# Pooled attention and a top-1 expert layer: a third of a tile between a transfer and its first split

## The chip, the cores and the metric

The kernel runs on one core of one Trainium2 chip. A core has TensorE (PE in the profile), VectorE (DVE), ScalarE (ACT), GpSimd (POOL) and SyncE (SP, which here only issues DMAs). Each of them works through its own queue in order, and waits at an instruction whose inputs or buffers aren't ready. The metric is the device time of the kernel in microseconds. Before the change the median of three runs is 2689.65 us (2684.49 to 2690.37).

## The reference

```python
def _attn_ref(q, kv, w_sr):                     # q: 4 x 12288 x 128, kv: 4 x 384 x 32 x 128
    kv_pool = kv.reshape(B, H // 4, 4, W // 4, 4, C).mean(axis=(2, 4))
    k = v = kv_pool.reshape(B, -1, C) @ w_sr    # 768 keys a batch, which are the values too
    s = (q @ k.transpose(0, 2, 1)) / np.sqrt(C)
    a = np.exp(s - s.max(-1, keepdims=True))
    a /= a.sum(-1, keepdims=True) + 1e-09
    return a @ v

def _moe_ref(x, w_gate, w1, w2):                # x: the 49152 rows above, 8 experts, 128 -> 1024 -> 128
    logits = x @ w_gate
    expert_idx = np.argmax(logits, axis=1)
    ...
    for e in range(E):
        mask = expert_idx == e
        h = np.maximum(x[mask] @ w1[e], 0.0)
        out[mask] = gate_w[mask, None] * (h @ w2[e])
    return out
```

`gate_w` is the softmax of the logits at the chosen expert.

## The kernel before

The 49152 query rows are worked off in 96 tiles of 512 rows, 24 a batch. To keep float32 accuracy every matmul is done as three in the type float32r (`mm3`, lines 219 to 221): each operand is split into a high part (a cast, `high`, line 213, on ACT) and a low part (source minus high, `low`, line 216, on DVE or POOL).

A tile goes through these steps:

- `load` (SP, four DMAs, line 685) and `turn_q` (DVE) bring the queries in and transpose them; `high_q` (ACT) and `low_q` (POOL) split them.
- Four times, for 128 rows each: `scores` (PE, 768 columns, into one of two places in PSUM in turn, so that it needs the exponential of the scores two before), `maxima` (DVE, line 719), `exps` (ACT, line 730), `turn_p` (DVE, 32 x 32 blocks transposed, line 742, into `pb`).
- `move_p` (SP, four DMAs, line 752) finishes the transposition of the probabilities by moving blocks between partitions, from `pb` to `pt`. There are two `pt` buffers, so the transfer of tile i waits for the last `values` matmul of tile i-2 as well as for the last `turn_p` of its own tile.
- Three times, for a third of the keys each: `high_p` (ACT, tile `pth`, 128 x 1024) and `low_p` (POOL, into `pt` itself).
- `values` 0 to 5 (PE), accumulated in one bank, of which 0 and 1 need the first third, 2 and 3 the second, 4 and 5 the last. `high_x` (ACT) and `low_x` (DVE) split the result, `xh` and `xl`.
- `logits` (PE), `diag` (ACT, tile `lgd`), and for pairs of tiles a row of small instructions on DVE, POOL and ACT for the choice of the expert and the gate (`route`; `df` at line 408, `dn` at 434, `se` at 448, `sx` at 461, `sb` at 475).
- Eight times: `first` (PE, an eighth of the hidden units, in one of three free banks), `high_h` (ACT, a relu, tile `hh`, three buffers), `low_h` (DVE, tile `hlow`), `second` (PE, accumulated in one bank).
- `turn_y` (DVE), `scale_y` (POOL, tile `yo`) and `put` (SP, four DMAs, line 904).

All rows of a batch first go through the expert that most rows of its first tile chose. For three of the four batches POOL scatters the row numbers to lists by indirect DMA (line 664), and two passes near the end work off 128 rows each of the other experts. While a batch runs, the keys of the next are pooled, projected and split, in six tiles of its 24 (`keys`; 18 such tiles for batches 1 to 3).

The order on PE, ACT, DVE and POOL is written out by numbers. Each step of tile i is recorded at a time 16 i + an offset, the program is emitted in the order of these times, and each engine's queue has that order. The offsets are in `AT` (line 30); they set an order only, and one unit is a sixteenth of a tile. An offset such as 34.98 therefore means that `values` 0 of a tile stands among the work of two tiles later. SP isn't in that order by hand: a scheduler places its DMAs.

Of the kernel before, what the change touches and what calls it, by code (L numbers as in the profile page):

```python
# [27 lines left out]


AT = {  # L30
    "turn_q": -17.69, "high_q": -7.6, "low_q": -5.97, "maxima": 1.36, "exps": 2.18, ("scores", 0): -0.86,
    ("scores", 1): 3.8, ("scores", 2): 7.89, ("scores", 3): 12.08, ("first_p", 0): 6.32, ("first_p", 1): 4.1,
    ("first_p", 2): 4.74, ("first_p", 3): 5.1, ("first_p", 4): 5.32, ("first_p", 5): 7.4, "first_high": 0.5,
    "first_low": 1.3, "first_values": 2.69, "turn_p": 2.9, "move_p": 17.32, ("high_p", 0): 20.23,
    ("high_p", 1): 22.63, ("high_p", 2): 24.99, "low_p": 1.26, ("values", 0): 34.98, ("values", 1): 37.95,
    ("values", 2): 38.94, ("values", 3): 39.96, ("values", 4): 45.78, ("values", 5): 47.57, "high_x": 0.58,
    "low_x": 1.04, "logits": 3.4, "diag": 3.87, "route": 5.41, "step": 0.4, "scale_exp": 2.92, "scale": 2.84,
    "apart": 7.77, "spread": 9.4, "keep_s": 10.53, ("first", 0): 66.35, ("first", 1): 67.88,
    ("first", 2): 68.93, ("first", 3): 70.9, ("first", 4): 73.89, ("first", 5): 74.05, ("first", 6): 76.9,
    ("first", 7): 78.27, "high_h": 0.48, "low_h": 1.51, "second": 4.29, "turn_y": 0.9, "scale_y": 2.68,  # L40
    "put": 4.98, "cut": -4.95,
}


# [1155 lines left out]
```

## Time and profile before

| | |
|---|---|
| median of three runs | 2689.65 us |
| the profiled execution | 2689.08 us |
| its span, first to last instruction | 2687.4 us |
| instructions | 29654 |
| ACT, idle in front of `pth` | 661.8 us over 279 |
| POOL, idle in front of `pt` | 613.2 us over 279 |
| DMA, mean busy share of q1 (SP's) | 42.4% |
| one `pt` transfer, issue to landing, median | 6.5 us |

The profile names a group of instructions by line, engine and tile, `pth<-pt` being what it writes and what it reads. Idle time of an engine is put down to whoever released it. Times of queues (SPq) are issue times. The granted clock is a share of full speed, for TensorE alone.

### The profile page before, as it was taken

How to read it: one execution, taken by the hardware profiler on the slowest of the kernel's cores; microseconds unless marked ns; L12 is line 12 of the kernel's file. 1: busy time of each engine (PE TensorE's matmuls, PEld its weight loads, DVE VectorE, ACT ScalarE, POOL GpSimd, SP SyncE). 2: the span in 40 equal slices, each digit the busy share in tenths (PEclk: the TensorE clock that was granted, in tenths of full speed). 3: DMA queues.
4: the chain of work that ended last, by engine and by line, in shares of the span. 5: the costliest groups of instructions: out<-in, count | busy, mean ns of one | idle time of the engine just before them, and what ended most of it. 6: DMA issues, size and time to landing. Idle time of an engine off the chain costs nothing.

```text
span 2687.4 us, 29654 instructions
## 1 busy us (share of the span) xinstructions
PE 2220.8 (83%) x9316; PEld 1782.4 (66%) x9316; DVE 1718.2 (64%) x2658; ACT 1332.4 (50%) x2630; POOL 1295.0 (48%) x1157
## 2 busy tenths in 40 slices
PE   3788888788878888878888888887888888887887
PEld 2576766666667676667666667676766767676765
DVE  5565667775666566766576657676667666666654
ACT  2555454555455544545444545554545454554543
POOL 1133454565565545555465545455547454434432
PEclk9898989998989898999889898899888889898998
DMA  7333335444353443554435343544343434435230
GB/s 139 75 75 83 80 78 118 109 98 85 74 123 72 86 79 78 120 109 90 91 87 108 67 92 66 107 112 100 87 92 81 85 72 83 114 71 127 59 83 17
DMA packets 497650, 239.89 MB, mean 89 GB/s; under 512 B 427440, under 2 KB 433714, under 8 KB 497488
## 3 DMA queue, kind: packets, MB, share of 16 engines
q1 hardware_dynamic: 488144, 237.69, 42.4%
q0 software_dynamic: 9344, 0.26, 0.3%
q8 instruction: 74, 1.21, 0.2%
q14 instruction: 88, 0.72, 0.1%
HBM read 59.97 MB, written 31.92 MB: 34 GB/s over the span
## 4 chain that ended last, share of the span: by engine, by line
PE 46%; DMA 23%; SPq 12%; ACT 8%; DVE 6%; issue 4%; POOL 0%; ACTq 0%; DVEq 0%; POOLq 0%
DMA pt<-pb 23%; PE ps L219 16%; PE ps L220 15%; PE ps L221 15%; SPq L752 12%; ACT pth L213 3%; ACT prob L730 3%; ACT hh L863 2%; DVE hlow L867 1%; DVE nmax L719 1%; DVE pb L742 1%; DVE half L256 1%; DVE se L448 1%; DVE df L408 0%; DVE pk L536 0%
## 5 line engine op out<-in xcount | busy, mean ns | idle before, releaser
L216 POOL TENSOR_TENSOR pt<-pt,pth 128x1024 fp32r<-128x1024 f32 x279 | 665.7, 2386 | 613.2 <-ACT pth L213 572.3
L867 DVE SCALAR_TENSOR_TENSOR hlow<-ps,hh 128x512 fp32r<-128x512 f32 x768 | 514.6, 675 | 654.6 <-ACT hh L863 653.6
L213 ACT CAST pth<-pt 128x1024 fp32r<-128x1024 f32 x279 | 293.4, 1052 | 661.8 <-DMA pt<-pb 588.7
L863 ACT ACTIVATE hh<-ps 128x512 fp32r<-128x512 f32 x768 | 451.7, 600 | 309.8 <-PE ps L221 298.3
L219 PE MATMUL ps<-kh,qh 128*128 128x512 f32 (+1 forms) x768 | 290.4, 378 | 302.8 <-ACT prob L730 301.6
L742 DVE STREAM_TRANSPOSE pb<-prob 128x768 f32<-128x768 f32 x372 | 362.0, 973 | 123.7 <-ACT prob L730 115.7
L730 ACT ACTIVATE prob<-ps,nmax 128x768 f32<-128x768 f32 x384 | 355.4, 926 | 132.2 <-DVE nmax L719 131.8
L719 DVE TENSOR_REDUCE nmax<-ps 128x1 f32<-128x768 f32 x384 | 363.1, 946 | 83.1 <-PE ps L221 82.8
L219 PE MATMUL ps<-xh,wt 128*128 128x512 f32 x768 | 329.4, 429 | 91.6 <-DVE hlow L867 85.1
L219 PEld LDWEIGHTS ps<-kh,qh 128*128 128x128 f32 x768 | 156.1, 203 | 365.5 <-ACT prob L730 341.4
L219 PE MATMUL ps<-hh,wt 128*128 128x512 f32 x768 | 336.3, 438 | 3.2 <-ACT hh L863 3.2
L220 PE MATMUL ps<-hlow,wt 128*128 128x512 f32 x768 | 333.8, 435 | 2.4 <-DVE hlow L867 2.4
L221 PE MATMUL ps<-hh,wt 128*128 128x512 f32 x768 | 329.9, 430 | 0.0
L664 POOL DMA_INDIRECT lists<-row,dst x288 | 289.5, 1005 | 55.8 <-issue 51.6
L220 PE MATMUL ps<-xl,wt 128*128 128x512 f32 x768 | 316.1, 412 | 0.0
L221 PE MATMUL ps<-xh,wt 128*128 128x512 f32 x768 | 314.3, 409 | 0.0
L895 POOL TENSOR_TENSOR yo<-yb,sb 128x512 f32<-128x512 f32 x96 | 100.5, 1047 | 443.0 <-DVE yb L890 242.3
L220 PE MATMUL ps<-kl,qh 128*128 128x512 f32 (+1 forms) x768 | 273.4, 356 | 0.0
L221 PE MATMUL ps<-kh,ql 128*128 128x512 f32 (+1 forms) x768 | 272.1, 354 | 0.1
L219 PEld LDWEIGHTS ps<-xh,wt 128*128 128x128 f32 x768 | 158.3, 206 | 137.4 <-DVE hlow L867 93.6
L221 PE MATMUL ps<-pth,vl 128*128 128x512 f32 x558 | 239.7, 430 | 0.0
L219 PE MATMUL ps<-pth,vh 128*128 128x512 f32 x558 | 238.6, 428 | 0.0
(203 smaller groups left out, 3279.2 us busy)
## 6 DMA issues: line engine op xcount, KB each, us to landing
pt<-pb SPq DMA_DIRECT2D x372, 384.0 KB, 6.5
raw<-in_kv_dram SPq DMA_DIRECT2D x96, 256.0 KB, 3.6
qb<-in_q_dram SPq DMA_DIRECT2D x384, 64.0 KB, 2.3
out_dram<-yo SPq DMA_DIRECT2D x384, 64.0 KB, 2.8
raw<-in_moe_w_dram SPq DMA_DIRECT2D x12, 512.0 KB, 4.6
lists<-row,dst POOLq DMA_INDIRECT x288, 2.2
kvs<-kh SPq DMA_DIRECT2D x4, 384.0 KB, 2.3
kvs<-kl SPq DMA_DIRECT2D x4, 384.0 KB, 2.5
```

What stands on the lines that cost most here:

```text
L213: nc.scalar.copy(out=dst, in_=src)
L216: eng.tensor_tensor(out=dst, in0=src, in1=h.bitcast(F32), op=ALU.subtract)
L219: nc.tensor.matmul(out=ps, lhsT=wh, rhs=xh, start=start, stop=False)
L220: nc.tensor.matmul(out=ps, lhsT=wh, rhs=xl, start=False, stop=False)
L221: nc.tensor.matmul(out=ps, lhsT=wl, rhs=xh, start=False, stop=stop)
L664: put = nc.gpsimd.indirect_dma_start(out=lists, out_offset=bass.IndirectOffsetOnAxis(ap=state["dst", b, c][:, n : n + 1].bitcast(U32), axi ...
L719: nc.vector.tensor_reduce(out=nmax, in_=own["s", a], op=ALU.max, axis=AX.X, negate=True)
L730: nc.scalar.activation(out=by_key(prob) if i < FIRST else prob, in_=split_keys(own["s", a]) if i < FIRST else own["s", a], func=AF.Exp, bi ...
L742: nc.vector.transpose(out=own["pb"][:, :, :, a, :].rearrange("p c b t -> p b c t"), in_=own["prob", a].rearrange("p (b c t) -> p b c t", c ...
L752: nc.sync.dma_start(out=dst[:, g], in_=src[g * SQ : (g + 1) * SQ])
L863: nc.scalar.activation(out=hh, in_=own["hp", f], func=AF.Relu)
L867: nc.vector.scalar_tensor_tensor(out=hl, in0=own["hp", f], scalar=0.0, in1=own["hh", f].bitcast(F32), op0=ALU.max, op1=ALU.subtract,)
```

## The change

It changes numbers in `AT` and nothing else; the function bodies and the number of instructions stay. The offsets of the three `high_p` go up by 4.28, 5.05 and 3.79 sixteenths of a tile:

```diff
-    "turn_q": -17.69, "high_q": -7.6, "low_q": -5.97, "maxima": 1.36, "exps": 2.18, ("scores", 0): -0.86,
+    "turn_q": -17.69, "high_q": -7.6, "low_q": -7.35, "maxima": 1.36, "exps": 2.04, ("scores", 0): 0.0,
...
-    "first_low": 1.3, "first_values": 2.69, "turn_p": 2.9, "move_p": 17.32, ("high_p", 0): 20.23,
-    ("high_p", 1): 22.63, ("high_p", 2): 24.99, "low_p": 1.26, ("values", 0): 34.98, ("values", 1): 37.95,
...
+    "first_low": 1.3, "first_values": 2.69, "turn_p": 3.06, "move_p": 17.26, ("high_p", 0): 24.51,
+    ("high_p", 1): 27.68, ("high_p", 2): 28.78, "low_p": 6.6, ("values", 0): 34.68, ("values", 1): 37.36,
```

On ACT, before, in the middle of the program, from the exponential of the first 128 rows of a tile (`prob_11717`) to the last split of the tile ahead (all three splits read `pt_11719`):

```order
L730 ACTIVATE prob_11717,sums_11716<-ps_152,nmax_11709 128x768
L863 ACTIVATE hh_11735<-ps_152 128x512
L385 COPY lgd_11542<-ps_152 32x128 x4
L213 CAST pth_11759<-pt_11719 128x1024
L863 ACTIVATE hh_11761<-ps_152 128x512
L863 ACTIVATE hh_11776<-ps_152 128x512
L730 ACTIVATE prob_11784,sums_11716<-ps_152,nmax_11768 128x768
L213 CAST pth_11795<-pt_11719 128x1024
L863 ACTIVATE hh_11813<-ps_152 128x512
L213 CAST qh_11833<-qt_11686 128x512
L213 CAST pth_11837<-pt_11719 128x1024
```

The same tile on ACT after the change, up to the first of its splits and a little beyond (they read `pt_11709` here, and the other two follow four rows further down):

```order
L730 ACTIVATE prob_11720,sums_11719<-ps_152,nmax_11714 128x768
L863 ACTIVATE hh_11734<-ps_152 128x512
L385 COPY lgd_11541<-ps_152 32x128 x4
L863 ACTIVATE hh_11761<-ps_152 128x512
L863 ACTIVATE hh_11778<-ps_152 128x512
L730 ACTIVATE prob_11782,sums_11719<-ps_152,nmax_11766 128x768
L863 ACTIVATE hh_11799<-ps_152 128x512
L213 CAST qh_11822<-qt_11674 128x512
L213 CAST pth_11824<-pt_11709 128x1024
L863 ACTIVATE hh_11851<-ps_152 128x512
L730 ACTIVATE prob_11853,sums_11719<-ps_152,nmax_11838 128x768
```

The first split stood ahead of the `hh` of expert steps 1, 2 and 3, of the second exponential and of `qh`; now it stands behind them all, and ahead of the `hh` of step 4 and the third exponential.

On POOL, before, from one tile's output rows (`yo`) to the last low part of a tile of probabilities (`pt_10550`):

```order
L895 TENSOR_TENSOR yo_10603<-yb_10581,sb_10567 128x512
L216 TENSOR_TENSOR pt_10550<-pt_10550,pth_10594 128x4x256
L664 DMA lists_75<-row_8116,dst_9711 397312x2
L216 TENSOR_TENSOR pt_10550<-pt_10550,pth_10620 128x4x256
L216 TENSOR_TENSOR ql_10670<-qt_10514,qh_10651 128x512
L664 DMA lists_75<-row_8116,dst_9711 397312x2
L216 TENSOR_TENSOR pt_10550<-pt_10550,pth_10655 128x4x256
```

On POOL after the change, from the gate's `sx` through the low parts of one tile (`pt_10743`) to the output rows:

```order
L461 TENSOR_TENSOR sx_10919<-row_9991,quad_123 128x16 x2
L664 DMA lists_75<-row_8110,dst_9715 397312x2
L216 TENSOR_TENSOR pt_10743<-pt_10743,pth_10858 128x4x256
L216 TENSOR_TENSOR pt_10743<-pt_10743,pth_10906 128x4x256
L664 DMA lists_75<-row_8110,dst_9715 397312x2
L216 TENSOR_TENSOR pt_10743<-pt_10743,pth_10922 128x4x256
L895 TENSOR_TENSOR yo_11021<-yb_11019,sb_10969 128x512
```

The three low parts stood behind `yo`, with the small rows of the gate and `ql` between them; now they stand together, behind `sx` and ahead of `yo`.

On PE, `values` 5 of a tile moves ahead of `second` 5 and of the next tile's `scores` 0, and `values` 4 stands right in front of it; `values` 1 and 2 follow each other, `second` 7 goes behind `values` 0 and `first` 7 ahead of `second` 4. On DVE, `xl` moves from behind the first maximum of a tile to ahead of it, right behind the last `hlow`. On SP, whose rows follow from the others, a piece of the query load now stands between the transfer and the output rows:

```order
L752 DMA pt<-pb 128x1x768 x4
L685 DMA qb<-in_q_dram 32x16x32
L904 DMA out_dram<-yo 32x16x32 x4
L685 DMA qb<-in_q_dram 32x16x32 x3
```

Before, the four pieces of the query load stood together behind the output rows.

More of the change, by code (lines that the diff above doesn't have):

```diff
@@ L30 @@
 AT = {
-    "turn_q": -17.69, "high_q": -7.6, "low_q": -5.97, "maxima": 1.36, "exps": 2.18, ("scores", 0): -0.86,
-    ("scores", 1): 3.8, ("scores", 2): 7.89, ("scores", 3): 12.08, ("first_p", 0): 6.32, ("first_p", 1): 4.1,
+    "turn_q": -17.69, "high_q": -7.6, "low_q": -7.35, "maxima": 1.36, "exps": 2.04, ("scores", 0): 0.0,
+    ("scores", 1): 3.8, ("scores", 2): 8.16, ("scores", 3): 12.5, ("first_p", 0): 6.32, ("first_p", 1): 4.1,
     ("first_p", 2): 4.74, ("first_p", 3): 5.1, ("first_p", 4): 5.32, ("first_p", 5): 7.4, "first_high": 0.5,
-    "first_low": 1.3, "first_values": 2.69, "turn_p": 2.9, "move_p": 17.32, ("high_p", 0): 20.23,
-    ("high_p", 1): 22.63, ("high_p", 2): 24.99, "low_p": 1.26, ("values", 0): 34.98, ("values", 1): 37.95,
[L36 to L41, printed above, removed]
+    "first_low": 1.3, "first_values": 2.69, "turn_p": 3.06, "move_p": 17.26, ("high_p", 0): 24.51,
+    ("high_p", 1): 27.68, ("high_p", 2): 28.78, "low_p": 6.6, ("values", 0): 34.68, ("values", 1): 37.36,
+    ("values", 2): 37.37, ("values", 3): 39.33, ("values", 4): 46.57, ("values", 5): 46.84, "high_x": 0.58,
+    "low_x": 1.04, "logits": 3.4, "diag": 4.52, "route": 6.37, "step": 0.4, "scale_exp": 2.67, "scale": 3.11,
+    "apart": 4.33, "spread": 8.01, "keep_s": 8.68, ("first", 0): 66.2, ("first", 1): 67.88,
+    ("first", 2): 68.9, ("first", 3): 70.6, ("first", 4): 73.48, ("first", 5): 74.05, ("first", 6): 76.52,
+    ("first", 7): 78.07, "high_h": 0.57, "low_h": 1.51, "second": 5.06, "turn_y": 0.97, "scale_y": 1.03,
+    "put": 6.25, "cut": -5.08,
 }
```

## The prediction

> **What bounds the kernel now.** I read the page's busy shares first, then the list of waits, then the chain of work that ended last, then one tile of it in windows.
>
> ```profile
> PE 2220.8 (83%) x9316; PEld 1782.4 (66%) x9316; DVE 1718.2 (64%) x2658; ACT 1332.4 (50%) x2630; POOL 1295.0 (48%) x1157
> ...
> PE 46%; DMA 23%; SPq 12%; ACT 8%; DVE 6%; issue 4%; POOL 0%; ACTq 0%; DVEq 0%; POOLq 0%
> ```
>
> No engine is full, and 35% of the chain is one transfer: the DMA and SyncE's queue (SPq) that issues it. The list of waits says who stands still for it.
>
> ```profile
> ACT pth L213 <- DMA pt<-pb: 588.7, 93, 8.0
> ...
> PE ps L219 <- ACT prob L730: 301.6, 87, 5.7
> PE ps L219 <- DVE hlow L867: 95.9, 21, 6.4
> ...
> POOL sx L461 <- DVE row L452: 16.7, 9, 5.5
> ```
>
> ACT stands 588.7/93 = 6.3 us in front of the first split of nearly every tile (93 of 96 tiles have such a transfer), with its other work queued behind it, and so PE stands 301.6/87 = 3.5 us, mostly in front of scores that need an exponential. One round of the chain shows how this repeats (start, length, what):
>
> ```profile
> 1329.09 0.33 SPq L752
> 1329.46 0.60 SPq L752
> 1330.11 2.39 SPq L752
> 1332.55 6.48 DMA pt<-pb
> 1339.12 1.05 ACT pth L213
> 1340.22 0.47 issue
> 1340.68 0.59 ACT hh L863
> 1341.28 0.89 ACT prob L730 x2
> 1342.21 0.58 PE ps L219
> ```
>
> At 1329.09 the last values matmul of tile i-2 ends and frees the buffer `pt`. Four issues and the transfer take until about 1339.0, that is **9.9 us** after it. Only then may ACT split, relu and exponentiate, and PE goes on at 1342.21. The same round in windows (length, then busy time and count of PE, PEld, DVE, ACT, POOL; then granted clock):
>
> ```profile
> 1329.10:1338.10 9.00, 9.00 (x41) 7.13 (x40) 4.69 (x8) 3.09 (x8) 1.05 (x1) 1.00 0.81 176
> 1338.10:1342.20 4.10, 0.12 (x1) 0.00 (x0) 1.34 (x3) 3.05 (x6) 1.96 (x1) 0.92 0.58 100
> 1342.20:1348.40 6.20, 6.19 (x16) 5.03 (x17) 4.97 (x11) 4.08 (x7) 5.27 (x5) 0.50 0.00 0
> 1348.40:1356.15 7.75, 7.75 (x37) 6.40 (x37) 6.80 (x10) 3.19 (x6) 5.81 (x6) 1.00 0.11 17
> ```
>
> PE is full for 9 us, idle for 4, then full **at half the clock** for 6.2 us (16 matmuls instead of some 30), then full again. The idle time costs twice: itself, and 3.1 us of slow clock behind it. Not every gap does that (idle time in brackets, and the rows behind it):
>
> ```profile
> 133.36 0.58 PE L219 MATMUL ps<-kh,qh 128*128 128x256 f32 x1 [4.21 <-ACT prob L730]
> 342.35 0.38 PE L219 MATMUL ps<-kh,qh 128*128 128x256 f32 x1 [2.70 <-ACT prob L730]
> ...
> 342.81 0.40 PE L219 MATMUL ps<-pth,vh 128*128 128x512 f32 x1
> ```
>
> After 4.21 us the matmul of 256 columns took 0.58 us, after 2.70 us 0.38, and the next one 0.40, its full-clock length. So a tile without this stall takes PE 27.05 - 3.99 - 3.1 = **20.0 us**. The tile interval now is read from the first and last of 92 equal instructions, one a tile (tiles 4 to 95):
>
> ```profile
> 108.28 1.28 POOL L216 TENSOR_TENSOR ql<-qt,qh 128x512 fp32r<-128x512 f32 x1 [16.43 <-ACT qh L213]
> ...
> 2574.50 1.27 POOL L216 TENSOR_TENSOR ql<-qt,qh 128x512 fp32r<-128x512 f32 x1
> ```
>
> 91 intervals in 2466.2 us: 27.10 us each.
>
> **The change, part by part.** It adds and removes no instruction; durations stay those of these groups:
>
> ```profile
> L216 POOL TENSOR_TENSOR pt<-pt,pth 128x1024 fp32r<-128x1024 f32 x279 | 665.7, 2386 | 613.2 <-ACT pth L213 572.3
> L867 DVE SCALAR_TENSOR_TENSOR hlow<-ps,hh 128x512 fp32r<-128x512 f32 x768 | 514.6, 675 | 654.6 <-ACT hh L863 653.6
> L213 ACT CAST pth<-pt 128x1024 fp32r<-128x1024 f32 x279 | 293.4, 1052 | 661.8 <-DMA pt<-pb 588.7
> L863 ACT ACTIVATE hh<-ps 128x512 fp32r<-128x512 f32 x768 | 451.7, 600 | 309.8 <-PE ps L221 298.3
> ...
> L742 DVE STREAM_TRANSPOSE pb<-prob 128x768 f32<-128x768 f32 x372 | 362.0, 973 | 123.7 <-ACT prob L730 115.7
> L730 ACT ACTIVATE prob<-ps,nmax 128x768 f32<-128x768 f32 x384 | 355.4, 926 | 132.2 <-DVE nmax L719 131.8
> L719 DVE TENSOR_REDUCE nmax<-ps 128x1 f32<-128x768 f32 x384 | 363.1, 946 | 83.1 <-PE ps L221 82.8
> ```
>
> And of PE's steps, with six matmuls of 512 columns between these two starts at full clock:
>
> ```profile
> 1329.61 0.39 PE L219 MATMUL ps<-xh,wt 128*128 128x512 f32 x1
> ...
> 1331.01 0.39 PE L377 MATMUL ps<-xh,wgs 128*128 128x512 f32 x1
> ```
>
> 1.40/6 = 0.233 us, so 0.70 for an expert step or a values step, 0.47 for logits, and 1.05 for a scores step (three of 512 and three of 256 columns).
>
> *The first split behind more of ACT's work.* Count PE's new order from V, the end of the last values step, which releases the transfer. Ahead of ACT's split now stand `hh` of expert step 3 and `qh`, and that `hh` takes one of three buffers, freed by second step 0. Until its end PE does second 5, scores 0, second 6, first 0, logits, values 0, second 7, scores 1, first 1 and 2, values 1 and 2, first 3, second 0: eleven steps of 0.70, logits, and two scores: 7.7 + 0.47 + 2.1 = 10.3 us. Then `hh` 0.60 and `qh`, of the same shape, 0.60: the split stands ready at V + 11.5, and its data has been there since V + 9.9. **The wait of 6.3 us goes**, with 1.6 us to spare. Were the data later, ACT has another 0.9 us: the split done at V + 12.5, the `hh` behind it needs first 4, which ends at V + 13.4 (behind values 3, scores 2 and second 1). That `hh` is wanted by second 4 only 4.6 us later, for 1.3 us of `hh` and `hlow`: 3.3 us. PE feels a landing only 5.8 us late. What the landing can do:
>
> ```profile
> DMA to landing us min/median/max: 4.5/6.5/9.2
> ```
>
> 2.7 us late at the most, as measured now. SP's queue changes too: one piece of the q load stands between the transfer and the output rows, and one ahead of the next transfer, 0.6 us of issue by the second row of the chain. Cover: the 5.8 us.
>
> *Transposes ahead of the transfer.* It also waits for the last `pb`. From scores 3 to V, PE has first 6, first 7, second 4, values 4 and 5: 3.5 us. DVE needs the maximum, 0.95, then `hlow` 0.68 and `qt` (by its columns two thirds of a `pb`, 0.65) beside ACT's 0.93 of exponential, then `pb` 0.97: 3.2 us. About equal, and some 1.3 us late where a routing row of that length (`se`, quoted below; every second tile) pushes DVE; same cover.
>
> *What is late next.* `xh` and `xl` of the same V take 0.6 + 0.7 us (shapes of `hh` and `hlow`), but `xl` now stands behind that `pb` and one more `hlow`: at the worst V + 1.3 + 0.7 + 0.7 = V + 2.7, while PE reaches logits at V + 3.15 (second 5, scores 0, second 6, first 0). It is the tightest place, 0.5 us. I charge **0.8 us a tile** for it and like places. Ends: 0, by this count, and 2.7, the gap above that left the clock up; I stay nearer 0, since PE had no gap in the 9.00 and 7.75 us, in which it also waits for three engines.
>
> *POOL.* The three low parts now run behind each other, behind `sx`, later in the tile. `sx` needs DVE's `se`: first 4 ends 12.7 us after scores 0, `hh` 0.6, exponential 0.93, `pb` 0.97, `hlow` 0.68, `se` 1.29: 17.2; the first low part then ends at 19.6, and values 0 comes one tile on, at 20.0 + 2.9 = 22.9. Cost 0, with 3.3 us of cover for the small rows and scatters between. The low parts ahead of `yo` put an output off by two of them, 4.8 us, for which only SP waits.
>
> *Values, experts, routing a place to and fro on PE and DVE.* PE's sum of work is the same; a full PE hides them. Between -0.5 and +0.5 us a tile, inside the 0.8.
>
> *Denser tiles.* These windows are one interval each, a plain one and two in which keys of the next batch are made:
>
> ```profile
> 1155.45:1183.38 27.93, 23.35 (x102) 18.88 (x101) 20.00 (x31) 14.46 (x29) 14.13 (x12) 0.94 0.51 113
> 1183.38:1211.60 28.22, 23.56 (x106) 18.90 (x105) 22.00 (x35) 14.65 (x32) 19.79 (x28) 0.94 0.44 94
> ...
> 1266.21:1293.03 26.82, 22.61 (x94) 18.30 (x93) 16.81 (x27) 13.21 (x26) 13.66 (x12) 0.88 0.40 78
> ```
>
> DVE 16.8, ACT 13.2, POOL 13.7 fit under 20.8. In the 18 key tiles DVE has 20 to 22 us: **22.0** (ends 21.4 and 24). Some 15 tiles that pick experts or collect rows get 1.0 us more.
>
> **The sum**, against the profiled execution (2689.1 us around a span of 2687.4; the median 2689.65 is the same): 73 x 20.8 + 18 x 22.0 + 15 = 1929 us in place of 2466: -537. Behind the last interval two more stalls of 3 us go: -6. **2146 us.** As a check, the most that can go is PE's 301.6 + 95.9 idle, and the clock's share:
>
> ```profile
> core 0: 2687.4 us, clock 0.903
> ```
>
> 0.097 x 2687 = 261, in all 658; 543 is 83% of it.
>
> **A page's rule against it.** Two small DVE instructions vary widely (shortest, median, longest, ns):
>
> ```profile
> L448 DVE SCALAR_TENSOR_TENSOR se<-se,sum x52: 146/1294/3095, 86.0 to 2656.4; 128x8 f32<-128x8 f32 x44, 128x4 f32<-128x4 f32 x8
> ...
> L408 DVE TENSOR_TENSOR df<-l,mx x52: 182/1004/1136, 80.7 to 2652.1; 128x64 f32<-128x64 f32 x44, 128x32 f32<-128x32 f32 x8
> ```
>
> The Trainium skill, "SBUF — State Buffer", section "Who interferes with whom", says that a DVE instruction with two SBUF inputs and a GpSimd instruction that reads SBUF lock each other out for a whole instruction, which fits these spreads. With POOL's share rising from 13.7/27 to 13.7/21, more of these would meet.
>
> **The rivals.**
> - *Warm, but with gaps* of 1.5 to 2.7 us in each tile, from late `xl`, late low parts or a landing above 9 us. For: four queues that each run in order. Against: the margins above. 73 x 22.7 + 18 x 24 + 15 = 2104: **2320 us**. 20%.
> - *DVE held by POOL* in the dense tiles: both small rows at their longest add 0.9 us a tile; PE hides that in plain tiles (17.7 under 20.8), and 18 key tiles get 1.5: **2173 us**. 5%.
> - *The transfer still ends last*, because both queues are busier: a gap over 4 us brings the half clock back. It needs a landing 5.8 us late, 12.3 where 9.2 was the longest. At 25 us a tile, **2500 us**. 8%.
> - *Nothing moves*: the loop from V through the transfer to the next V would have to be 27 us in the new order as well. From the split through `hh`, `hlow`, second 4 and values 4 and 5 to V I count 9.9 + 1.0 + 0.6 + 0.7 + 2.1 = 14.3. **2690 us**, 3%.
> - *Slower*: POOL's first low part now waits behind `sx`, which waits for DVE (5.5 us at the longest above). If it comes over 3.3 us late, PE stops at values 0; from 4.0 us of stop the clock halves and costs 3.1 more, which together is all of the gain. That point is a lateness of 7.3 us in every tile. At 8.8 us: 20 + 5.5 + 3.1 = 28.6 a tile, **2826 us**. Against: only 9 such waits now, and `sx` in every second tile. 7%.
>
> **The numbers.** The forecast has 57%, on its own 2056 (no friction: 73 x 20.0 + 18 x 21.4, so -621, and -12 behind) to 2215 (1.5 us of friction, key tiles 23: 73 x 21.5 + 18 x 23 + 15). With the first two rivals the range 2056 to 2340 holds 82%. Faster by over 0.2%, about what a measurement here can tell from no change: 57 + 20 + 5 + 8 = 90%; within it 3%; slower 7%.
>
> **What would show it.** Right: ACT's wait for the transfer below 60 us in total, PE's for `prob` below 50, the clock at 0.98 or more, intervals near 20.8. Wrong at the split: that ACT wait stays in hundreds. Wrong at friction: PE waits for `hlow`, `xl` or POOL's `pt` of over 1 us a tile at full clock. Wrong altogether if PE's gaps above 4 us stay, whoever ends them.

## The result and the profile after

| | before | after |
|---|---|---|
| median | 2687.07 us (4 runs, 2679.82 to 2690.37) | **2134.35 us** (4 runs, 2132.34 to 2135.63) |
| ratio | | 0.7945, 95% interval 0.7926 to 0.7965 |
| span of the profiled execution | 2687.4 us | 2133.2 us |
| tiles 4 to 95, interval | 27.10 us | 21.11 us |

The change took 553 us off. The forecast was 2146 us. The tile interval is read as in the prediction, from the first and last of 92 equal instructions:

```profile
110.91 1.28 POOL L216 TENSOR_TENSOR ql<-qt,qh 128x512 fp32r<-128x512 f32 x1 [16.99 <-ACT qh L213]
...
2031.59 1.29 POOL L216 TENSOR_TENSOR ql<-qt,qh 128x512 fp32r<-128x512 f32 x1 [4.51 <-issue]
```

The page of the changed kernel, busy shares and shares of the chain that ended last:

```profile
PE 2017.7 (95%) x9316; PEld 1654.3 (78%) x9316; DVE 1636.6 (77%) x2658; ACT 1310.5 (61%) x2630; POOL 1301.8 (61%) x1157
...
PE 78%; DVE 7%; issue 4%; DMA 3%; ACT 3%; POOL 2%; SPq 2%; POOLq 0%; DVEq 0%; ACTq 0%
```

PE's busy time went down by 203 us though its work is the same: its granted clock rose from 0.903 to 0.988. The page counts 29728 instructions in all, 74 more than before; the counts of each engine in the row above are unchanged. The transfer and SP's queue fell from 35% of the chain to 5%. The group of the splits, and the two waits of PE that were named, in the changed kernel:

```profile
L213 ACT CAST pth<-pt 128x1024 fp32r<-128x1024 f32 x279 | 283.3, 1051 | 4.1 <-DMA pt<-pb 4.1
```

```profile
PE ps L219 <- ACT prob L730: 37.5, 19, 4.6
...
PE ps L219 <- DVE hlow L867: 5.5, 5, 1.7
```

ACT's wait for the transfer fell from 588.7 us to 4.1, PE's for an exponential from 301.6 to 37.5. One tile in a window, with the same columns as in the prediction, and the clock of the whole execution:

```profile
1245.91:1266.06 20.15, 20.15 (x95) 16.67 (x94) 14.70 (x20) 13.17 (x26) 15.14 (x9) 1.00 0.53 105
```

```profile
core 0: 2133.2 us, clock 0.988
```

PE is busy in all of its 20.15 us. ACT's rows at both ends of the count show the place of the split: the window begins where the last values step releases `xh`, which is the prediction's V.

```profile
1245.91 0.59 ACT L213 CAST xh<-ps 128x512 fp32r<-128x512 f32 x1 [0.71 <-PE ps L221]
...
1256.90 0.61 ACT L213 CAST qh<-qt 128x512 fp32r<-128x512 f32 x1
1257.41 1.05 ACT L213 CAST pth<-pt 128x1024 fp32r<-128x1024 f32 x1
```

The split starts at V + 11.50 without a wait; how long its data had been there the profile doesn't tell.

### The profile page after: what moved, and what is told of

The parts are those of the page before. It is cut to its first block, busy times and chain, and to the rows that moved or that the text cites. A ratio compares the mean times of both kernels' runs of the same rounds, so it can differ in the third digit from the quotient of the medians.

```text
span 2133.2 us, 29728 instructions
## 1 busy us (share of the span) xinstructions
PE 2017.7 (95%) x9316; PEld 1654.3 (78%) x9316; DVE 1636.6 (77%) x2658; ACT 1310.5 (61%) x2630; POOL 1301.8 (61%) x1157
## 4 chain that ended last, share of the span: by engine, by line
PE 78%; DVE 7%; issue 4%; DMA 3%; ACT 3%; POOL 2%; SPq 2%; POOLq 0%; DVEq 0%; ACTq 0%
PE ps L219 25%; PE ps L221 25%; PE ps L220 25%; DVE hlow L867 1%; DVE half L256 1%; DVE nmax L719 1%; ACT prob L730 1%; DMA pt<-pb 1%; SPq L752 1%; PE ps L378 1%; PE ps L377 1%; DVE wt L216 1%; DVE pb L742 1%; DMA raw<-in_kv_dram 1%; DMA raw<-in_moe_w_dram 1%
## 5 line engine op out<-in xcount | busy, mean ns | idle before, releaser
L219 PE MATMUL ps<-xh,wt 128*128 128x512 f32 x768 | 308.3, 401 | 4.8 <-DVE hlow L867 4.6
L219 PE MATMUL ps<-hh,wt 128*128 128x512 f32 x768 | 309.3, 403 | 0.0
L221 PE MATMUL ps<-xh,wt 128*128 128x512 f32 x768 | 306.0, 398 | 0.0
L220 PE MATMUL ps<-xl,wt 128*128 128x512 f32 x768 | 304.6, 397 | 0.0
L221 PE MATMUL ps<-hh,wt 128*128 128x512 f32 x768 | 303.6, 395 | 0.0
L219 PE MATMUL ps<-kh,qh 128*128 128x512 f32 (+1 forms) x768 | 266.9, 348 | 38.6 <-ACT prob L730 37.5
L220 PE MATMUL ps<-hlow,wt 128*128 128x512 f32 x768 | 303.0, 395 | 0.0
L220 PE MATMUL ps<-kl,qh 128*128 128x512 f32 (+1 forms) x768 | 263.0, 342 | 0.0
L216 POOL TENSOR_TENSOR ql<-qt,qh 128x512 fp32r<-128x512 f32 x96 | 124.2, 1294 | 184.7 <-issue 89.2
L220 PE MATMUL ps<-pt,vh 128*128 128x512 f32 x558 | 218.2, 391 | 1.2 <-POOL pt L216 1.1
L221 PE MATMUL ps<-pth,vl 128*128 128x512 f32 x558 | 219.3, 393 | 0.0
L219 PE MATMUL ps<-pth,vh 128*128 128x512 f32 x558 | 219.2, 393 | 0.0
```

Source lines behind the costliest of these rows:

```text
L216: eng.tensor_tensor(out=dst, in0=src, in1=h.bitcast(F32), op=ALU.subtract)
L219: nc.tensor.matmul(out=ps, lhsT=wh, rhs=xh, start=start, stop=False)
L220: nc.tensor.matmul(out=ps, lhsT=wh, rhs=xl, start=False, stop=False)
L221: nc.tensor.matmul(out=ps, lhsT=wl, rhs=xh, start=False, stop=stop)
```

## The experiments

Times are medians of four runs, ratios are to the kernel before on the same chip. The five rows below the change take it apart.

| kernel | us | ratio, 95% interval |
|---|---|---|
| the change | 2134.35 | 0.7945 (0.7926 to 0.7965) |
| splits alone | 2264.42 | 0.8421 (0.8391 to 0.8450) |
| all but the splits | 2505.82 | 0.9306 (0.9275 to 0.9338) |
| first split behind two `hh` | 2533.52 | 0.9429 (0.9396 to 0.9462) |
| first split behind an exponential too | 2305.87 | 0.8571 (0.8543 to 0.8599) |
| splits and POOL's low parts | 2135.10 | 0.7960 (0.7922 to 0.7998) |
| the change, low parts close again | 2173.41 | 0.8106 (0.8088 to 0.8123) |
| the change, one more piece | 2214.44 | 0.8246 (0.8210 to 0.8284) |
| the change, two more pieces | 2426.27 | 0.9051 (0.9033 to 0.9068) |
| the same, columns turned | 2386.53 | 0.8882 (0.8840 to 0.8923) |
| before, two more pieces | 3013.96 | 1.1253 (1.1228 to 1.1278) |
| the change, weights on POOL | 2117.24 | 0.7909 (0.7890 to 0.7929) |
| the same, columns turned | **2105.78** | 0.7843 (0.7808 to 0.7878) |

### The splits alone

```diff
-    ("high_p", 0): 20.23, ("high_p", 1): 22.63, ("high_p", 2): 24.99,
+    ("high_p", 0): 24.51, ("high_p", 1): 27.68, ("high_p", 2): 28.78,
```

> The kernel before with the three offsets of the first-to-last split alone (24.51, 27.68, 28.78); values, expert steps and the distance of POOL's low parts (1.26) stay as before. Theory 'place': the place of ACT's splits makes the whole gain, so 2130 to 2200 us, ACT's wait for the transfer under 60 us in total, clock over 0.98. Rival 'fit': the other offsets are needed to make use of it, so over 2300 us, with PE waiting elsewhere for over 1.5 us a tile.

2264.42 us, where the kernel before had 2691.79 on the same chip: 427 of the 553 us by the splits alone, between the two theories. What is missing shows in PE's waits of this kernel:

```profile
PE ps L468 <- POOL sx L461: 57.8, 28, 2.8
PE ps L612 <- DVE xtot L607: 34.4, 11, 5.7
...
PE ps L219 <- ACT prob L730: 21.2, 14, 3.4
```

PE waits for the spread of the gates (`sx`) and for the ranks (`xtot`) more than for exponentials. POOL's rows at one such place:

```profile
999.90 2.40 POOL L216 TENSOR_TENSOR pt<-pt,pth 128x1024 fp32r<-128x1024 f32 x1
...
1002.53 2.35 POOL L216 TENSOR_TENSOR pt<-pt,pth 128x1024 fp32r<-128x1024 f32 x1
1005.05 1.08 POOL L664 DMA_INDIRECT lists<-row,dst  x1 [0.17 <-issue]
1006.16 0.74 POOL L593 TENSOR_TENSOR xoh<-xoh,np 128x256 f32<-128x256 f32 x1
1006.84 0.39 POOL L461 TENSOR_TENSOR sx<-row,quad 128x16 f32<-128x16 f32 x2
```

The low parts follow their splits at a distance of 1.26 and so moved with them, to the front of `xoh`, which the ranks need, and of `sx`. A row of DVE is late beside them too, and PE stopped for the ranks:

```profile
1000.73 4.43 DVE L587 TENSOR_TENSOR xoh<-chosen,order 128x256 f32<-128x256 f32 x1
```

```profile
1008.62 0.17 PE L612 MATMUL ps<-xtot,upper 128*128 128x8 bf16 x1 [5.13 <-DVE xtot L607]
```

DVE's `xoh` comes ahead of POOL's and has two inputs in SBUF. It took 4.43 us and ended 0.3 us behind POOL's second low part; in the changed kernel the longest of its twelve took 0.45 us.

### The splits and POOL's low parts

The kernel above, with the low parts further behind:

```diff
-    "low_p": 1.26,
+    "low_p": 6.6,
```

> The kernel before with the three splits moved as in the change and POOL's low parts a third of a tile behind them (distance 6.6), all else as before. With the splits alone PE waited 57.8 us for sx (line 461, on POOL behind the low parts, to spread the gates) and 34.4 us for the ranks, and its clock fell to 0.962. Theory 'POOL order': the rest of the gain lies in where the low parts stand, so that these two waits fall under 25 us in total and the time to 2150 to 2200 us. Rival 'values': it lies in the order of values and expert steps on PE, so the time stays within 1% of the 2264 us.

2135.10 us, the time of the whole change and 15 us under what the theory said. These four numbers of the table are the change; the other new offsets add nothing that can be measured to them. PE's waits for `sx` and for the ranks fell to 8.0 and 1.3 us, and the clock is 0.988 again:

```profile
ACT pth L213 <- DMA pt<-pb: 57.1, 52, 2.7
...
PE ps L468 <- POOL sx L461: 8.0, 3, 2.8
```

ACT still waits for the transfer here, 52 times, and it costs nothing that can be measured: what counts is what stands behind the wait.

### All but the splits

The changed kernel with the three `high_p` back at 20.23, 22.63 and 24.99.

> The changed kernel with the three splits back at 20.23, 22.63, 24.99 and all else as changed. Theory 'place': the wait of some 6 us a tile returns and with it the half clock: 2600 to 2720 us, clock 0.90 to 0.92. Rival 'fit': the fitted values and expert steps keep a part of the gain, 2300 to 2500 us.

2505.82 us, 6 us above the range of 'fit'. ACT's wait for the transfer is back, as theory 'place' says, but a third of the gain is there, as 'fit' says:

```profile
ACT pth L213 <- DMA pt<-pb: 514.1, 93, 8.2
```

Of values and expert steps this is what can be argued: V now comes ahead of second 5 and scores 0, so that PE has those 1.75 us beside the transfer. It was not tried by itself, and the kernel has POOL's low parts at their new distance as well. The gains overlap: 427 and 186 us are more than 553. With the splits and the low parts moved the rest is worth nothing, as the kernel above shows.

### The first split, step by step

The kernel before, with one number changed, to 21.5 (behind the `hh` of steps 1 and 2) and to 22.3 (behind the second exponential too):

```diff
-    ("high_p", 0): 20.23,
+    ("high_p", 0): 21.5,
```

> The kernel before with the first split alone moved from 20.23 to 21.5, that is behind the relu of expert steps 1 and 2, but still ahead of the second exponential. Theory 'place': scores 3 need that exponential, so PE still stops there until the transfer lands; 2580 to 2690 us, PE's wait for prob still over 250 us. Rival 'share': every instruction freed from behind the split brings its part, two of five, so about 2470 us.

```diff
-    ("high_p", 0): 20.23,
+    ("high_p", 0): 22.3,
```

> The kernel before with the first split alone moved from 20.23 to 22.3, that is behind the second exponential as well, a step of one more instruction on ACT. Theory 'place': PE now has all work up to the third exponential, some 8 to 10 us, while the transfer takes 9.9; its gap falls under 2.7 us and the clock stays up: 2150 to 2300 us, clock over 0.97. Rival 'share': three of five parts of the gain, about 2360 us, with the clock still near 0.93.

2533.52 us, less than theory 'place' allowed and more than 'share', with PE's wait of 279.0 us as 'place' said. Then 2305.87 us, 6 us above what 'place' said and with the clock that it asked for. On ACT the two differ by one place, so one exponential that no longer queues behind a waiting split is worth 228 us. PE's wait for `prob` in the first kernel, then in the second beside its clock:

```profile
PE ps L219 <- ACT prob L730: 279.0, 118, 4.6
```

```profile
PE ps L219 <- ACT prob L730: 108.7, 96, 3.4
```

```profile
core 0: 2305.3 us, clock 0.980
```

PE still waits 1.1 us in every tile, but at a nearly full clock. The wait of 3.5 us of the kernel before went with a clock of 0.903. That is the double price of the prediction, taken off in two steps.

### A longer transfer

To see how much cover the new place has, more pieces of the same size go from `pb` to scratch in HBM, issued behind the first piece of each `pt` transfer:

```diff
             for g in range(QT):
                 nc.sync.dma_start(out=dst[:, g], in_=src[g * SQ : (g + 1) * SQ])
+                for k in range(2 if g == 0 else 0):
+                    nc.sync.dma_start(out=spare[i % 2, k], in_=src[k * SQ : (k + 1) * SQ])
```

> The changed kernel with two more pieces of a transfer of the same size (to scratch in HBM) issued behind the first piece of each pt transfer, so that the rest lands some 3 to 5 us later. Theory 'margin': PE feels a landing only when it is 5.8 us late: 2130 to 2160 us, though ACT may wait 1 to 3 us a tile for the transfer. Rival: the transfer is close to being the bound again, each us late is a us a tile: 2134 + 93 x 3 to 5 = 2410 to 2600 us.

> The kernel before with the same two more pieces. Theory: its loop runs through the transfer, so each us of landing is a us a tile: 2687 + 93 x 3 to 5 = 2960 to 3150 us. Rival: the transfer is hidden in part and only its end is waited for, under 2800 us.

The kernel before became 334 us slower than its own base of 2680 (3.6 us a tile), as a loop through the transfer must. The changed kernel became 292 us slower, as its rival said, and theory 'margin' falls. Two rows of the changed kernel with two pieces tell where PE stood, and what for:

```profile
1350.20 0.89 ACT L731 ACTIVATE prob<-ps,nmax 128x768 f32<-128x768 f32 x1
```

```profile
1351.24 0.58 PE L220 MATMUL ps<-kh,qh 128*128 128x256 f32 x1 [2.32 <-ACT prob L731]
```

Counted from 0, the exponential is number 2 of its tile, and the 256 columns are the first of scores 3. By the rule in the section on the kernel, scores 3 need exponential 1 only. But a scores place is 768 columns, one bank and a half, so the two places share a bank, and those 256 columns lie in it. In the kernel before it was the same: PE had done the 512 columns of scores 2 and stopped at its 256. The Trainium skill, "PSUM — Partial Sum Buffer", section "PSUM bank collisions raise a hardware error ⚠️", says that two engines may not be in the same bank and quadrant at once, which is why a program must wait here. The trace agrees: PE waited 2.32 us in this row, until that exponential.

Two tests of this, one with a single piece, one with two and the order of columns turned for scores 1 and 3:

> The changed kernel with one more piece in place of two. With two the transfer took 14.9 us from its first issue in place of 9.9, and the time rose by 292 us. New theory 'shared bank': scores 3 begin with the 256 columns that lie in a bank with scores 2, so they need exponential 2, which ends 0.5 us before PE is there; PE then feels a landing 1.6 + 0.9 + 0.5 = 3.0 us late. One piece brings about 2.5 us: 2134 to 2165 us. Old theory (5.8 us of cover, something else was lost with two pieces, such as bandwidth): half of the 292 us, about 2280 us.

```diff
-            for hs in (slice(0, cut), slice(cut, NK)):
+            for hs in (slice(0, cut), slice(cut, NK))[:: -1 if side else 1]:
```

> The changed kernel with two more pieces, and for scores 1 and 3 the 512 columns ahead of the 256 that share a bank with the scores before. Theory 'shared bank': PE meets the wait 0.7 us later, with work done in between, so 0.7 us a tile less or a little more with the clock: 2300 to 2370 us in place of 2426. Rival (scores wait for the exponential two before, whatever the order of columns): 2426 us within 0.5%.

Turned, 2386.53 us: 40 us less, where the theory forecast 56 to 126 and the rival none. Scores 3 of this kernel now do their 512 columns before they stop, at the 256:

```profile
1312.05 0.39 PE L220 MATMUL ps<-kh,qh 128*128 128x512 f32 x1
...
1314.90 0.39 PE L220 MATMUL ps<-kh,qh 128*128 128x256 f32 x1 [1.99 <-ACT prob L731]
```

So the shared bank is a part of it, and a smaller one. One piece cost 80 us, more than the new theory said and less than the old one. The chain of this kernel says what both lacked (start, length, what):

```profile
1260.78 0.04 ACT pth L214
...
1263.70 1.64 ACT pth L214 x2
...
1265.47 0.61 ACT hh L866
...
1266.71 0.31 DVE qt L690
...
1267.34 0.94 DVE pb L743
...
1268.34 0.56 SPq L753
...
1274.73 6.81 DMA pt<-pb
...
1281.64 0.04 ACT pth L214
```

No PE is in it. From the first split ACT works on through exponentials 2 and 3 with two more splits between, DVE makes the last `pb` behind an `hlow` and a `qt`, and this releases the next transfer: 7.5 us to 1268.28, and 13.3 us of transfer with one more piece. Together they are 20.86 us, above the 20.1 us that PE needs for a tile; 0.8 us in 93 tiles are most of the 80. Without the piece, with the prediction's 9.9 us for the transfer, it is 7.5 + 9.9 = 17.4 us. **The changed kernel's cover is therefore about 2.7 us**, not 5.8. This is an estimate from single tiles of two kernels. The changed kernel itself shows that the loop is near: there too the last `pb`, and not V (at 1245.91), releases the transfer.

```profile
1245.07 0.94 DVE L742 STREAM_TRANSPOSE pb<-prob 128x768 f32<-128x768 f32 x1
```

```profile
1246.08 5.88 SPq L752 DMA_DIRECT2D pt<-pb  x4
```

With two pieces this loop and the shared bank meet: ACT's exponential 3 waits for the scores 3 that PE does late and, from the row at 1351.24 on, at half the clock.

### POOL's low parts close to the splits again

The changed kernel with `"low_p": 1.26`.

> The changed kernel with POOL's low parts right behind their splits again (distance 1.26 in place of 6.6). Theory: POOL then works beside the routing rows, and the instruction se (two inputs in SBUF) is long again, median over 0.8 us where the changed kernel has 0.15; plain tiles have room on DVE for it, so 2130 to 2165 us. Rival 'lock binds': DVE is late for hlow and xl in every second tile, PE waits for them over 1 us a tile, 2200 us or more.

2173.41 us, and not as the theory said, nor as its rival: `se` stays short (median 152 ns), and PE hardly waits for `hlow` (2.9 us). The 39 us lie at the 12 places where rows are collected:

```profile
PE ps L612 <- DVE xtot L607: 53.8, 12, 6.5
```

In the changed kernel this wait is 7.1 us. The ranks need `xoh` from POOL, which stands behind the low parts there. And DVE's own `xoh`, which POOL's needs, is held beside the low parts again (shortest, median, longest, ns):

```profile
L587 DVE TENSOR_TENSOR xoh<-chosen,order x12: 360/2373/5058, 274.8 to 2141.6; 128x288 f32<-128x288 f32 x4, 128x256 f32<-128x256 f32 x4, 128x224 f32<-128x224 f32 x4
```

In the changed kernel these are 359, 417 and 451 ns. How the 39 us divide between POOL's order and this row was not tried.

### The weights' low parts on POOL

When a batch ends, the weights of the next expert are split. In the changed kernel DVE and POOL met at one of these places (rows of both, the first is DVE's):

```profile
617.46 5.45 DVE L216 TENSOR_TENSOR wt<-raw,wt 128x512 fp32r<-128x512 f32 x1
```

```profile
616.45 2.38 POOL L216 TENSOR_TENSOR pt<-pt,pth 128x1024 fp32r<-128x1024 f32 x1
618.76 1.30 POOL L216 TENSOR_TENSOR wt<-raw,wt 128x512 fp32r<-128x512 f32 x1
620.00 2.35 POOL L216 TENSOR_TENSOR pt<-pt,pth 128x1024 fp32r<-128x1024 f32 x1
622.52 1.26 POOL L664 DMA_INDIRECT lists<-row,dst  x1 [0.17 <-issue]
```

An instruction that takes 0.7 us elsewhere took 5.45, until the third of POOL's was over, and PE stopped 4.55 us behind it, with the half clock after:

```profile
624.86 0.58 PE L219 MATMUL ps<-kh,qh 128*128 128x256 f32 x1 [4.55 <-ACT prob L730]
```

```diff
-        low(wt[:, 2 * n + 1, cs], wf[:, cs], wt[:, 2 * n, cs], nc.vector if c else nc.gpsimd)
+        low(wt[:, 2 * n + 1, cs], wf[:, cs], wt[:, 2 * n, cs], nc.gpsimd)
```

> The changed kernel with the low parts of all four weight pieces of a batch on POOL, none on DVE. In the changed kernel one of these took DVE 5.45 us beside POOL's low parts, and PE stopped 4.55 us behind it, once in each of three batches. Theory 'lock': that stop and the half clock behind it go, 12 to 25 us in all: 2110 to 2125 us. Rival: the time was POOL's work itself, which now grows by 1.3 us twice a batch: no change or up to 10 us slower, 2134 to 2145 us.

2117.24 us, as forecast. By the times that is 17 us, by the ratios to each kernel's base 10 us, and the two intervals just overlap. The tile intervals of the profiled executions bear out the larger: their sum fell from 1920.7 to 1903.6 us, 12 us of it where a batch changes. With the columns of scores 1 and 3 turned as well:

> The changed kernel with the weights' low parts on POOL (2117 us) and the columns of scores 1 and 3 turned as well. In plain tiles PE is full already and gains nothing; the 22 us of waits for an exponential that are left may shrink by 0.7 us each, some 10 us with the clock: 2105 to 2117 us. Rival: no effect or up to 5 us slower, since the maximum of the turned scores waits as long as before.

2105.78 us, the fastest kernel of this study, 1.3% under the change.

## Why the prediction was right, point by point

- *The wait of 6.3 us goes, with its half clock.* Right in both halves: 4.1 us of that wait are left in the whole program, the clock is 0.988, and the split stands at V + 11.50 where the count said 11.5. The experiments bear the mechanism out: the splits alone bring 427 us, and one exponential of them 228.
- *The sum.* The 91 intervals take 1920.7 us (1929 forecast). Outside them the span lost 8.7 us (6 forecast): 11.3 behind the last, while the first starts 2.6 later. The terms were worse than the sum. Plain tiles take 20.15 and 19.9 us in turn: the friction of 0.8 us a tile isn't there, 58 us too much. Key tiles take 20.7 to 21.0, not 22.0, but the one of each batch in which rows are collected too takes 26. And the some 15 tiles charged with 1.0 us were priced far too low: the two at the change of a batch take 24.6 and 27.9 to 30.0, and eight near the end, beside the two passes of the other experts, 21.9 to 25.4. The errors cancel: that the sum came within 12 us is luck.
- *PE feels a landing only 5.8 us late.* Wrong. Two things were left out: the bank that both scores places share, and the loop through ACT's last exponential, `pb` and the transfer, which holds no PE at all. I had looked at that `pb` as one lateness of 1.3 us, not as a loop. The run with one more piece puts the cover at about 2.7 us.
- *POOL's move costs 0.* True of the whole change: POOL waits for DVE ahead of `sx` for 161.8 us in place of 16.7, and PE for the low parts only 1.1 us. But there is a reason for the move that the prediction lacked. The low parts must not stay close to the moved splits: with the splits alone they cost 129 us, and PE's waits show them at `sx` and the ranks. The place of the 'slower' rival, `sx` against the low parts on POOL, was right, and its direction was the other.
- *Values, experts, routing: within 0.5 us a tile.* Right: without them 2135.10 us.
- *DVE held by POOL.* Not in the routing rows of the changed kernel: `se` (line 448) fell from a median of 1.29 us to 0.15 and its longest to 0.16, though POOL's share rose.

```profile
L448 DVE SCALAR_TENSOR_TENSOR se<-se,sum x52: 146/152/161, 90.0 to 2102.2; 128x8 f32<-128x8 f32 x44, 128x4 f32<-128x4 f32 x8
```

With the splits and low parts alone it is long again, in a kernel that is as fast:

```profile
L448 DVE SCALAR_TENSOR_TENSOR se<-se,sum x52: 147/870/2830, 85.5 to 2100.0; 128x8 f32<-128x8 f32 x44, 128x4 f32<-128x4 f32 x8
```

So it is one of the other new offsets that shortens `se`, which one is open, and it gains nothing that can be measured. The lock that the Trainium skill's page "SBUF — State Buffer", section "Who interferes with whom", describes did cost time, at the weights, where the prediction had not looked, and it fits DVE's `xoh` where the low parts stand close to the splits.

## What to carry to other kernels

In a queue that runs in order, an instruction that waits for a transfer belongs behind everything that doesn't need it; the question is what stands behind it, and one exponential was worth 228 us here. When the instruction is moved, look at what moves along by a fixed distance on another engine (129 us here). And count every loop that closes through the transfer, also those in which the busiest engine has no part: they set how much cover is left.

## What was not expected of the hardware

A DVE instruction with two inputs in SBUF was held through three POOL instructions in a row, not one (5.45 us in place of 0.7). And no length of gap alone decides PE's clock: 2.70 us left it up in the kernel before, while in the changed kernel with two more pieces a gap of 2.32 us was followed by a 256-column matmul of 0.58 us and 512-column ones of 0.63.
